# Zero products ahead of the first load, markers on the loads of x and table d, and two engines for the first-stage copies

## The chip, the core and the metric

The program runs on one core of a Trainium2 chip. A core has a matrix engine (TensorE, PE in the profile, with its weight loads as PEld), VectorE (DVE), ScalarE (ACT), GpSimd (POOL) and SyncE (SP), each with a queue of its own that it works through in order. They meet through semaphores. SP, ACT and POOL can also issue DMAs; the transfers of all three run on the core's 16 DMA engines. The metric is the device time of one execution in microseconds. The kernel before took 459.18 us, the median of 3 runs (457.12 to 460.07).

## What is computed

Two blocks follow each other. The first filters a sequence in the frequency domain, for 8 batches of 2496 rows and 256 columns:

```python
X = np.fft.rfft(x, axis=1)
F = (filt_r + 1j * filt_i)[None, :, :]
Y = X * F
y = np.fft.irfft(Y, n=x.shape[1], axis=1)
```

The second takes the 19968 rows of y as tokens for 8 experts. Each token goes to the expert with the largest logit; an expert keeps the 80 of its tokens with the largest gate, and the rows of all others stay zero:

```python
logits = x @ w_gate
expert_idx = np.argmax(logits, axis=1)
gate_w = probs[np.arange(N), expert_idx]          # softmax of the logits
h = np.maximum(x[tok_idx] @ w1[e], 0.0)           # tok_idx: the kept tokens of expert e
out[tok_idx] = gate_w[tok_idx, None] * (h @ w2[e])
```

All data is fp32.

## The kernel before, in words

A transform of length 2496 = 39 x 64 is done in two stages of matrix products. For each batch b:

- `load_x` (line 295) brings one **chunk** of x, 4 column groups of 117 rows and 256 columns (468 KB, the last of a batch 234 KB), on SP's queue. A batch has NCH = 6 chunks; the pool has NX0 = 7 slots. `put_x` loads the next chunk in the list of all 48; before the loop it is called seven times, with the first part of table d between the sixth and the seventh.
- `stage1(b, k)` (line 304) multiplies two groups of a chunk by the table `wf_t` in four calls, tile `pa` (line 311), and ACT copies the result into `t1` (line 317). A batch has NB = 11 blocks k; a chunk feeds two. `put_s1` issues the next block in the list and, when a chunk has been read to its end, calls `put_x`, so that a new chunk is loaded as soon as TensorE is through with an old one.
- `transpose1(b, u)` (line 319) turns part of `t1` through tile `pt`, and ACT copies it to `t2` (line 327). u runs over NU = 10.
- `stage2(b, u)` (line 331) multiplies `t2` by table `d_t` (tile `pb`, line 336). Two multiplications on DVE (line 344) take the filter `ft`, and two additions on POOL (line 351) combine them.
- `turn(b, u)` (line 355) turns the result back and adds the gate columns through `gi` (tile `py`, line 360). ACT copies the spectrum to SBUF (line 376), and after every second u it stores 512 KB of it to `yf` in DRAM (line 379). For the first two batches the spectrum also stays in SBUF, and only a fallback for unusual inputs reads their `yf`. DVE moves the gate columns (lines 382, 383).

The filter comes in five parts v. `load_filter(v, half)` (line 270) fetches 2 x 128 rows with indirect DMAs that POOL issues (line 273), `sign_filter(v)` (line 281) flips signs on ACT, and `turn_filter(v, k)` (line 284) turns a half through tile `pf` (line 289), which DVE copies to `ft` (line 291).

The order on each engine is written out by hand under `tc.manual_schedule()` (line 797); instructions stand on each queue in the order of the calls. First come the loads and all eleven blocks of batch 0, with parts 1 to 3 of table d loaded after blocks 2, 5 and 8. Then the first filter part is turned, two transposes and two blocks of batch 1 follow, and part 4 of d. The main loop (line 869) runs over v = 10 b + u in steps: `stage2` of step v, a filter part if it is due, `transpose1` of step v + 2, one block of the first stage (a second one when u = 3), zero rows of the output from batch 1 on, and `turn` of step v - 2. On POOL, a copy to `mark` (line 831) holds back the gathers of filter parts 1 and 2 until the last chunk of batch 0 is there.

Three PSUM slots (pool `fps`, tag f) serve `pa`, `pt` and `pb`, one (`pkps`) serves `pf`, two serve `py`. After the loop come the picking of tokens, the second transform of the picked rows and the experts; the change does not touch them.

## Time and profile before

| | before |
|---|---|
| median of 3 runs | 459.18 us (457.12 to 460.07) |
| the profiled execution | 462.53 us, span 460.7 us |
| mean granted TensorE clock | 0.983 |
| PE busy | 433.7 us (94%) |
| PEld busy | 410.1 us (89%) |
| ACT busy | 222.4 us (48%) |
| DVE busy | 188.4 us (41%) |
| POOL busy | 180.1 us (39%) |
| DMA | 109.96 MB, mean 239 GB/s |

The profile is one execution, recorded by the hardware. A busy line in slices cuts the span into 40 equal parts and gives the busy share of each in tenths. A row of the stretches gives the same in microseconds for a chosen time. A row of the waits reads: engine, tile and line that waited, what ended the wait, microseconds in total, times, the longest. A row of the timeline gives the start, the length, the engine, the line, the operation, the tiles written and read, and how many of them are merged. "remote" stands for a wait whose end the profile cannot give to an instruction. The ends of products are modelled, and some records can be missing. An fp32 product of one tile leaves two records, so a block of the first stage has eight.

### The profile page before, as it was taken

To read this page: it belongs to the slowest core of one execution; us is meant where nothing else is said; L and a number is where in the kernel's file an instruction comes from. 1 tells how busy PE (TensorE), PEld (TensorE's weight loads), DVE (VectorE), ACT (ScalarE), POOL (GpSimd) and SP (SyncE) were. 2 spreads that over 40 slices of the span, in tenths; PEclk is the share of its full clock that TensorE was granted. 3 is DMA by queue.
4 is the path that set the end of the run, shared out by engine and by line. 5 is a ranking of instruction groups with operands and counts; after the bars stand their busy time and mean duration, and the time that the engine had idled before them with its cause. 6 is when DMAs were issued, how large, how long until landed. Compare 5 with 4: busy or idle time off the path is not lost. (4 is left out here: it accounts for less than half of the span.)

```text
span 460.7 us, 8667 instructions
## 1 busy us (share of the span) xinstructions
PE 433.7 (94%) x3380; PEld 410.1 (89%) x3380; DVE 188.4 (41%) x550; ACT 222.4 (48%) x363; POOL 180.1 (39%) x246
## 2 busy tenths in 40 slices
PE   4969999999999999999999999999999999999990
PEld 4869899999999999999999998888888888888870
DVE  2134554544664454674545789568220000101100
ACT  2836667666676766667666754442123321111110
POOL 8468434343344433444443465420654002211210
PEclk9979999999999999999999999999999999999996
DMA  7996647877877887787894222797988991999200
GB/s 217 275 269 178 202 122 239 278 245 237 272 220 248 281 267 241 234 270 235 305 400 184 82 105 92 273 364 275 349 333 317 373 333 38 362 372 371 59 19 11
DMA packets 39477, 109.96 MB, mean 239 GB/s; under 512 B 5073, under 2 KB 14608, under 8 KB 38658
## 3 DMA queue, kind: packets, MB, share of 16 engines
q1 hardware_dynamic: 28688, 76.41, 50.7%
q10 hardware_dynamic: 6178, 21.04, 11.5%
q0 software_dynamic: 4560, 11.86, 7.9%
q8 instruction: 29, 0.48, 0.4%
q14 instruction: 22, 0.18, 0.1%
HBM read 68.97 MB, written 43.20 MB: 243 GB/s over the span
## 5 line engine op out<-in xcount | busy, mean ns | idle before, releaser
L351 POOL TENSOR_TENSOR p<-p,p 128x256 f32<-128x256 f32 x154 | 110.1, 736 | 138.6 <-DVE p L344 120.7
L344 DVE TENSOR_TENSOR p<-pb,ft 128x512 f32<-128x512 f32 x160 | 102.2, 681 | 19.5 <-PE pb L336 9.7
L317 ACT COPY t<-pa 128x480 f32<-128x480 f32 x88 | 87.0, 1001 | 27.8 <-PE pa L311 21.6
L311 PE MATMUL pa<-wf_t,x 117*128 117x120 f32 x704 | 93.6, 282 | 6.2 <-DMA x<-in_x_dram 6.0
L311 PEld LDWEIGHTS pa<-wf_t,x 117*128 117x128 f32 x704 | 87.9, 198 | 6.4 <-DMA x<-in_x_dram 6.0
L336 PE MATMUL pb<-d_t,t 128*128 128x128 f32 x640 | 86.2, 278 | 3.7 <-DVE p L344 3.5
L360 PE MATMUL py<-gi,p 128*128 128x136 f32 x640 | 87.8, 280 | 1.3 <-POOL p L351 0.7
L336 PEld LDWEIGHTS pb<-d_t,t 128*128 128x128 f32 x640 | 78.8, 193 | 4.7 <-issue 3.7
L360 PEld LDWEIGHTS py<-gi,p 128*128 128x128 f32 x640 | 79.8, 190 | 1.7 <-POOL p L351 1.0
L327 ACT COPY t<-pt 128x512 f32<-128x512 f32 x80 | 46.9, 587 | 67.1 <-PE pt L325 62.9
L508 PE MATMUL po<-yb,wt 128*128 128x256 f32 x240 | 56.6, 380 | 1.5 <-ACT wt L501 1.5
L508 PEld LDWEIGHTS po<-yb,wt 128*128 128x128 f32 x240 | 43.4, 190 | 6.5 <-ACT wt L501 1.7
L382 DVE COPY z<-py 128x16 f32<-128x16 f32 x60 | 11.2, 187 | 91.7 <-ACT ysp L376 57.9
L325 PE MATMUL pt<-ident,t 128*128 128x128 f32 x320 | 48.5, 274 | 0.0
L501 ACT COPY wt<-pw 128x512 f32<-128x512 f32 x39 | 22.8, 587 | 48.9 <-PE pw L496 42.5
L325 PEld LDWEIGHTS pt<-ident,t 128*128 128x128 f32 x320 | 38.0, 142 | 0.0
L376 ACT COPY ysp<-py 128x512 f32<-128x512 f32 x60 | 35.4, 590 | 0.0
L1153 PEld LDWEIGHTS ph<-xs,w 128*128 128x128 f32 x256 | 29.7, 192 | 1.7 <-DVE xs L1144 1.1
L1153 PE MATMUL ph<-xs,w 128*128 128x80 f32 x256 | 29.8, 274 | 0.8 <-DVE xs L1144 0.8
L1168 PE MATMUL po<-w,hT 128*80 128x256 f32 x128 | 28.8, 379 | 0.0
L1168 PEld LDWEIGHTS po<-w,hT 128*80 128x80 f32 x128 | 18.6, 150 | 7.5
L479 POOL DMA_INDIRECT gts<-rows_tbl,idxb x16 | 16.2, 1010 | 21.0 <-DVE idxb L695 16.7
(200 smaller groups left out, 315.6 us busy)
## 6 DMA issues: line engine op xcount, KB each, us to landing
out_dram<-zero_t SPq DMA_DIRECT2D x64, 312.0 KB
x<-in_x_dram SPq DMA_DIRECT2D x40, 468.0 KB
w<-in_moe_w_dram SPq DMA_DIRECT2D x16, 1024.0 KB
yf<-ysp ACTq DMA_DIRECT2D x30, 512.0 KB
yb<-yf SPq DMA_DIRECT2D x6, 2560.0 KB
yf<-ys ACTq DMA_DIRECT2D x10, 512.0 KB
x<-in_x_dram SPq DMA_DIRECT2D x8, 234.0 KB
d_t<-d_tbl SPq DMA_DIRECT2D x5, 256.0 KB
```

The costliest lines, as they stand in the source:

```text
L311: nc.tensor.matmul(out=ps[:, i, :, 2 * NS * cb:2 * NS * cb + 2 * NS], lhsT=xt[0:NJ * N1, (2 * k + i) % JC, 128 * cb:128 * cb + 128], rhs=w ...
L317: nc.scalar.copy(out=t1[:, 2 * k - h:2 * k - h + 2], in_=ps[:])
L325: nc.tensor.transpose(ps[:, i, cb, :], t1[:, a:a + 2, :].rearrange("p r n -> p (r n)"), ident[:])
L327: nc.scalar.copy(out=t2[:].rearrange("p i c -> p (i c)"), in_=ps[:].rearrange("p i c q -> p (i c q)"))
L336: nc.tensor.matmul(out=ps[:, cb, i], rhs=d_t[:, 2 * u + i, :], start=True, stop=True, lhsT=t2[:, i, 128 * cb:128 * cb + 128])
L344: nc.vector.tensor_tensor(out=pt, in0=ps[:].rearrange("p c s r q -> p (c s) r q"), in1=f.unsqueeze(2).to_broadcast([128, 2 * NDB, 2, NQ]), ...
L351: adder.tensor_tensor(out=yt[:, :, r, :], in0=yt[:, :, r, :], in1=pr[1][:, :, 1 - r, :], op=op)
L360: nc.tensor.matmul(out=ps[:, i, ZW * cb:ZW * cb + ZW], rhs=gi[:, cb, :], lhsT=yt[:, 2 * cb + i].rearrange("p r q -> p (r q)"), start=True, ...
L376: nc.scalar.copy(out=dst.rearrange("p s (h w) -> p s h w", h=2), in_=pv[:, :, :, 0:128])
L508: nc.tensor.matmul(pos[t][:, 0, 0:C], lhsT=wts[t, g // 2][:, g % 2, i, :], rhs=ybs[t][:, s, :], start=(s == 0), stop=(s == NS - 1))
L1153: nc.tensor.matmul(ph[:, fc // 4, fc % 4, 0:cap], lhsT=self.w1s[e][:, k, 128 * fc:128 * fc + 128], rhs=xs[:, k, :], start=(k == 0), stop=( ...
L1168: nc.tensor.matmul(po[0:cap, :], lhsT=hT[:, fc, :], rhs=self.w2s[e][:, fc, :], start=(fc == 0), stop=(fc == NFC - 1))
```

## The change

1. Line 113: a bf16 tile `warm` is set to zero by DVE as its first work, and TensorE multiplies it by itself nine times (128 x 512 results into one slot of `fps`) ahead of its first product of x.
2. In the first stage of batch 0, blocks 1, 4, 7 and 10 are copied by DVE instead of ACT.
3. The two small loads of the gate columns move from POOL's queue to ACT's, ahead of the loop; the mark on POOL waits for chunk 3 of batch 0 instead of the last.
4. A chunk of x is no longer loaded when a slot comes free. `put_x(v)` is called once in a step; it loads as many chunks as are free and due. Chunks 7 to 20 in the list have a step each before which they are not due. Up to step 19, DVE writes one element of the slot first (a marker), so that the DMA on SP's queue waits until DVE has come to that place in its order. Part 1 of d is loaded after block 7, parts 2 to 4 in steps 0, 2 and 4, each behind such a marker.
5. The first filter part gets its sign after block 6. Before the loop there is one block of batch 1 instead of two; step 7 does one more. `turn_filter` comes after the step's first-stage block instead of before the transpose, and its second half uses `fps`.
6. The five stores of batch 0's spectrum are issued in step u = 4 of batches 1 to 5 instead of during batch 0.

```diff
@@ -110,6 +110,8 @@
     consts = ctx.enter_context(tc.tile_pool(name="consts", bufs=1))
     dpool = ctx.enter_context(tc.tile_pool(name="dram", bufs=1, space=DRAM))
 
+    warm = consts.tile([128, 128], BF16, name="warm")
+    nc.vector.memset(warm[:], 0.0)
     ident = consts.tile([128, 128], F32, name="ident")
     make_identity(nc, ident)
     ident_bf = consts.tile([128, 128], BF16, name="ident_bf")
@@ -179,6 +181,7 @@
 
 
     NE, NY, NO = 3, 2, 3
+    NWARM = 9
     yf = {b: dpool.tile([128, NS, C], F32, name=f"yf_{b}") for b in range(B)}
     ypool = ctx.enter_context(tc.tile_pool(name="spec", bufs=NY))
     ysb = {}
@@ -283,7 +286,8 @@
 
         def turn_filter(v, k):
             f = fst[:, v]
-            ps = pkps.tile([128, 2, NDB, 128], F32, name=f"pf_{k}_{v}", tag="k")
+            ps = (fps if k else pkps).tile([128, 2, NDB, 128], F32, name=f"pf_{k}_{v}",
+                                           tag="f" if k else "k")
             for i in range(2):
                 for cb in range(NDB):
                     nc.tensor.transpose(ps[:, i, cb, :],
@@ -292,8 +296,10 @@
                 out=ft[k][:, 2 * v:2 * v + 2].rearrange("p u c s q -> p u c (s q)"),
                 in_=ps[:])
 
-        def load_x(b, ch):
+        def load_x(b, ch, hold=False):
             xt = xpool.tile([128, JC, C], F32, name=f"x_{b}_{ch}", tag="x")
+            if hold:
+                nc.vector.memset(xt[0:1, 0, 0:1], 0.0)
             ng = min(JC, NG - JC * ch)
             nc.sync.dma_start(
                 out=xt[0:NJ * N1, 0:ng, :],
@@ -314,7 +320,8 @@
                         rhs=wf_t[:], start=True, stop=True)
             h = k // (NB - 1)
             t1 = st["t1", b][:, :, h:h + N2 - 1].rearrange("p a (j g) -> p g j a", j=NJ)
-            nc.scalar.copy(out=t1[:, 2 * k - h:2 * k - h + 2], in_=ps[:])
+            copy = nc.vector.tensor_copy if b == 0 and k % 3 == 1 else nc.scalar.copy
+            copy(out=t1[:, 2 * k - h:2 * k - h + 2], in_=ps[:])
 
         def transpose1(b, u):
             t1 = st["t1", b]
@@ -352,6 +359,10 @@
                                     in1=pr[1][:, :, 1 - r, :], op=op)
             st["yt", b, u] = yt
 
+        def keep_spectrum(b, u):
+            src = st["ys"] if b >= NY else ysb[b][:, 2 * u - 2:2 * u + 2, :]
+            nc.scalar.dma_start(out=yf[b][:, 2 * u - 2:2 * u + 2, :], in_=src)
+
         def turn(b, u):
             yt = st.pop(("yt", b, u))
             ps = yps.tile([128, 2, 512], F32, name=f"py_{b}_{u}", tag="y")
@@ -374,9 +385,10 @@
             if b >= B - 2:
                 nc.scalar.copy(out=zz, in_=pv[:, :, :, 128:ZW])
             nc.scalar.copy(out=dst.rearrange("p s (h w) -> p s h w", h=2), in_=pv[:, :, :, 0:128])
-            if u % 2 == 1:
-                src = st["ys"] if b >= NY else ysb[b][:, 2 * u - 2:2 * u + 2, :]
-                nc.scalar.dma_start(out=yf[b][:, 2 * u - 2:2 * u + 2, :], in_=src)
+            if u % 2 == 1 and b > 0:
+                keep_spectrum(b, u)
+            if u == 4 and 0 < b < 6:
+                keep_spectrum(0, 2 * b - 1)
             if b < B - 2:
                 zz = zz[:, :, 0, :]
                 nc.vector.tensor_copy(out=zz, in_=pv[:, :, 0, 128:ZW])
@@ -798,29 +810,44 @@
             nc.scalar.dma_start(out=frow, in_=frow_dram.ap())
             nc.scalar.dma_start(out=wf_t, in_=wf_dram.ap())
             nc.scalar.dma_start(out=fsig, in_=fsig_dram.ap())
+            for cb in range(NDB):
+                nc.scalar.dma_start(out=gi[:, cb, 128:128 + E],
+                                    in_=moe_w_gate[128 * cb:128 * cb + 128, :])
+            pre = fps.tile([128, 4, 128], F32, name="warm_ps", tag="f")
+            for _ in range(NWARM):
+                nc.tensor.matmul(out=pre[:], lhsT=warm[:], start=True, stop=True,
+                                 rhs=warm[:].unsqueeze(1).to_broadcast([128, 4, 128]))
             xs = [(b, ch) for b in range(B) for ch in range(NCH)]
             s1 = [(b, k) for b in range(B) for k in range(NB)]
 
-            def put_x():
-                if xs:
-                    load_x(*xs.pop(0))
+            held = dict(zip(range(NX0, NX0 + 14),
+                            (-1, 0, 2, 3, 4, 5, 7, 8, 11, 13, 15, 16, 17, 18)))
+            free = [NX0]
+
+            def put_x(v):
+                while xs and free[0] and held.get(B * NCH - len(xs), -1) <= v:
+                    load_x(*xs.pop(0), hold=v < 20)
+                    free[0] -= 1
 
             def put_s1():
                 if s1:
                     b, k = s1.pop(0)
                     stage1(b, k)
                     if (2 * k + 2) % JC == 0 or k == NB - 1:
-                        put_x()
+                        free[0] += 1
 
             def load_d(g):
+                if g:
+                    nc.vector.memset(d_t[0:1, SG * g, 0:1], 0.0)
                 nc.sync.dma_start(out=d_t[:, SG * g:SG * g + SG, :],
                                   in_=d_dram.ap()[:, SG * g:SG * g + SG, :])
 
             for _ in range(NCH):
-                put_x()
+                load_x(*xs.pop(0))
             load_d(0)
             for _ in range(NX0 - NCH):
-                put_x()
+                load_x(*xs.pop(0))
+            free[0] = 0
             load_filter(0, 0)
             load_filter(0, 1)
             for t in (lg, zero_t, *zs, key, kt):
@@ -828,24 +855,23 @@
             nc.gpsimd.tensor_copy(out=gi[:, 0, 0:128], in_=ident[:])
             nc.gpsimd.tensor_copy(out=gi[:, 1, 0:128], in_=ident[:])
             mark = tpool.tile([1, 1], F32, name="mark")
-            nc.gpsimd.tensor_copy(out=mark[:], in_=st["x", 0, NCH - 1][0:1, 0, 0:1])
+            nc.gpsimd.tensor_copy(out=mark[:], in_=st["x", 0, NCH - 3][0:1, 0, 0:1])
             load_filter(1, 0)
-            nc.gpsimd.dma_start(out=gi[:, 0, 128:128 + E], in_=moe_w_gate[0:128, :])
-            nc.gpsimd.dma_start(out=gi[:, 1, 128:128 + E], in_=moe_w_gate[128:256, :])
             load_filter(1, 1)
             load_filter(2, 0)
             load_filter(2, 1)
             for k in range(NB):
                 put_s1()
-                if k in (2, 5, 8):
-                    load_d(k // 3 + 1)
-            sign_filter(0)
-            turn_filter(0, 0)
-            turn_filter(0, 1)
+                if k == 6:
+                    sign_filter(0)
+                if k == 7:
+                    load_d(1)
+                    put_x(-1)
+            for k in range(2):
+                turn_filter(0, k)
             for v in range(LEAD):
                 transpose1(0, v)
-                put_s1()
-            load_d(4)
+            put_s1()
             nlow = max(128 - cap, 8) // 8
             n0 = max(128 - cap, 8) // 8
             early = {67: [lambda: pick_edge(0, 6, 8, -1.0)],
@@ -870,10 +896,11 @@
                 b, u = divmod(v, NU)
                 if b < B:
                     stage2(b, u)
-                    if v + 2 < NU:
-                        if v % 2 == 1:
-                            sign_filter(v // 2 + 1)
-                        turn_filter(v // 2 + 1, v % 2)
+                    if v + 2 < NU and v % 2 == 1:
+                        sign_filter(v // 2 + 1)
+                    put_x(v)
+                    if v in (0, 2, 4):
+                        load_d(2 + v // 2)
                     if v < 4:
                         load_filter(3 + v // 2, v % 2)
                     elif v == 4:
@@ -883,8 +910,10 @@
                     if w < B * NU:
                         transpose1(*divmod(w, NU))
                     put_s1()
-                    if u == 3:
+                    if u == 3 or v == 7:
                         put_s1()
+                    if v + 2 < NU:
+                        turn_filter(v // 2 + 1, v % 2)
                     if b > 0:
                         put_zeros(1)
                 if v >= LATE:
```

## The prediction

> **What bounds the kernel now.** I read, in order, the page's slices, busy time by stretch, the waits of the first 110 us, the first-stage products in two stretches, and the timeline. In the slices each digit is tenths of 11.5 us.
>
> ```profile
> PE   4969999999999999999999999999999999999990
> PEclk9979999999999999999999999999999999999996
> ```
>
> TensorE (PE) is full from the fourth slice to the end, except the third and at the start; only the third shows a lower granted clock. The stretches say how much work each holds (length, then busy us and records of PE, weight load, DVE, ACT, POOL, then clock, DMA share, GB/s):
>
> ```profile
> 5.97:18.77 12.80, 12.80 (x90) 12.80 (x91) 0.00 (x0) 9.19 (x10) 7.42 (x14) 1.00 0.92 283
> 18.77:23.50 4.73, 3.75 (x32) 3.32 (x31) 1.38 (x2) 3.46 (x7) 3.82 (x5) 1.00 0.94 272
> 23.50:35.67 12.17, 8.31 (x50) 7.68 (x48) 3.77 (x6) 4.03 (x7) 7.71 (x10) 0.72 0.91 268
> 35.67:60.00 24.33, 23.66 (x203) 22.50 (x202) 12.69 (x28) 16.00 (x25) 15.30 (x21) 1.00 0.56 172
> 60.00:120.00 60.00, 60.00 (x533) 60.00 (x533) 28.99 (x74) 39.54 (x59) 24.35 (x35) 1.00 0.76 234
> ```
>
> The undisturbed rate is the last row's: 533 products in 60 us, 8.9 per us. Between 23.50 and 35.67 there are 50, 4.1 per us. So the kernel is bound by TensorE from about 60 us on, and what a change of the opening can win is what the opening loses against 8.9 per us. DMA is at 0.91 to 0.94 of its time from 6 to 36 us: the opening is crowded with loads. The waits (us in total, times, longest):
>
> ```profile
> PE pa L311 <- DMA x<-in_x_dram: 6.0, 1, 6.0
> PE pb L336 <- DVE p L344: 3.5, 1, 3.5
> DVE p L344 <- remote: 7.5, 1, 7.5
> POOL mark L831 <- DMA x<-in_x_dram: 4.6, 1, 4.6
> PE pf L289 <- ACT fst L281: 1.4, 3, 1.0
> ```
>
> PE waits 6.0 us for the first chunk of x, and 3.5 us (27.2 to 30.7) for VectorE (DVE), which itself stood 7.5 us for something the profile cannot name. ACT's next copy also restarted only then (29.38 against DVE's 29.26), though PE's records have the products done by 25.8. The mark, which waits for the last chunk of batch 0, shows when that landed: it ran at 16.18. The first-stage rows in two stretches, 6 to 11.5 and 12.5 to 18.6 (count, shortest/median/longest ns, first and last start):
>
> ```profile
> L311 PEld LDWEIGHTS pa<-wf_t,x x27: 288/333/338, 6.0 to 11.5; 117*128 117x128 f32 x27
> L311 PE MATMUL pa<-wf_t,x x26: 397/421/569, 6.0 to 11.5; 117*128 117x120 f32 x26
> L311 PE MATMUL pa<-wf_t,x x57: 275/275/275, 12.2 to 18.5; 117*128 117x120 f32 x57
> ```
>
> 26 starts in 5.5 us is 0.212 us each; 57 in 6.3 us is 0.1125. A block k has eight: 1.70 us early, 0.90 later. The page's clock says 1.0 in both, so it does not record the state before its first event.
>
> [...] 421 ns becomes 275 at about 11.7 us, and the 1-us stretches put the second half-clock spell at 28.8 to 35.6, 6.8 us[...]. [...] from 12 to 20 us, with almost no gather, SP's queue has 87.9% of DMA time; from 24 to 30, beside gathers, 59.5% against their 33.2%. [...]
>
> **The change, part by part,** against the profiled execution: 462.53 us, span 460.70.
>
> *Warm-up.* [...] They need only DVE's memset, so they run[...], in PE's 6.0 us of waiting: cost 0 while the cover stands. [...] Gain at most 26 x (0.212 - 0.1125) = 2.6 us, and 0 if zeros or the 1 us gap leave the clock cold.
>
> *x sets the pace.* With a warm clock eleven blocks need 9.9 us and would end at 15.9, but the last chunk lands at 16.2. The trace's semaphore records, which no view prints, put the chunks at 5.9, 7.3, 10.6, 13.1, 15.2 and 16.1. Two blocks per chunk: 10.7 to 12.5, 13.1 to 14.9, 15.2 to 17.0, the last to 17.9. Before, it ended at 18.77. So 0.9 of the 2.6 is left.
>
> *Copies by two engines.* ACT's copy takes 0.99 and ACT finished at 19.84; then came the sign (0.89), for which PE waited 1.0. Now block 10 is DVE's: the 128x512 copy of the same kind is 0.69, so 18.7, and the sign is done at block 6. Turns of the filter, 2 x 0.44, run to 18.8: transposes start at 18.8 instead of 20.86, 2.0 earlier. DVE was idle from 4.4 to 19.25, so four copies cost nothing.
>
> *Filters earlier.* The mark now waits for chunk 3 (13.1, not 16.18), and gathers start 3.2 us sooner. A gather is 131 KB per 1.27 us of POOL, 0.10 MB/us; 3.2 us of that is 0.33 MB, or 1.2 us at 0.28 MB/us, which x(1,0) lands later: 20.4 becomes 21.6. Transposes end at 19.7, so PE waits 1.9 and block (1,0) ends at 22.5. Second-stage product (0,0) starts at 22.5; before, 23.51, less the 0.89 of one first-stage block that now runs at step 7: 22.6. **Up to here 0.1 is won;** the start's gain turns into a wait for x.
>
> *The stall.* From product (0,0) to (0,2) before took 23.51 to 35.77, 12.3 us, for two steps of 0.89 + 0.44 + 0.44 + 0.89 = 2.66. Lost: 6.9, of which 3.5 idle, about 2.5 at half clock (30.7 to 35.6 at half), the rest waiting for sign and filter rows. After: filter rows are 3 us ahead and the turns follow the first-stage block, x(1,1) and its table part are 0.73 MB at the 0.18 left beside the gathers, 4 us, so about 25.6 against a need at 26.5. Product (0,2) at 27.8, like for like 34.9 before: **7.0 won.**
>
> *Steps 2 to 9.* 203 products at 8.9 per us are 22.8 us; the stretch took 24.33, 1.5 lost, mostly to turns behind the sign. I take half, 0.7 (0 to 1.5).
>
> *Held x.* A marker is a one-element memset (DVE's shortest rows, 0.14) behind that step's two multiplications. It waits for a slot already read, so nothing queues behind it on DVE but filter copies and z; on SP the next d load and zero store wait with it. Steps are 3.15 us:
>
> ```profile
> 60.07 1.05 PE L336 MATMUL pb<-d_t,t 128*128 128x128 f32 x8
> 61.39 1.05 PE L311 MATMUL pa<-wf_t,x 117*128 117x120 f32 x8
> 63.22 1.05 PE L336 MATMUL pb<-d_t,t 128*128 128x128 f32 x8
> ...
> 61.21 1.28 DVE L344 TENSOR_TENSOR p<-pb,ft 128x512 f32<-128x512 f32 x2
> ```
>
> Marker at about 62.6, need two steps on at 61.39 + 6.30 = 67.7: 5.1 us for the chunks issued at steps 15 and 16; for those of 11 and 13 an extra block makes it 6.1; others have three steps. The semaphore records have x landing 4.5 to 6.9 us after issue between 60 and 140 us, mostly 5.0 to 5.5. Cost 0 to 2 x 1.8 = 3.6; I take 0.4.
>
> *First spectrum later.* Five 512 KB stores (0.33 of ACT each) leave 45 to 75 us and come at u = 4 of batches 1 to 5: 0.52 MB per 32 us or 16 GB/s more on 234. Only the fallback reads them. Nothing, in the gaps of ACT (39.54 of 60 us busy); uncovered 5 x 0.33 = 1.6. Four table markers: nothing, their parts are needed two to four steps later.
>
> Sum: -7.0 - 0.7 + 0.4 = -7.3: 455.2 for the profiled execution. It stands 3.35 above the median, and the three runs lie 3 us apart, wider than the rest of the kernel can explain, so I take the stall and half clock (6.0) as varying, absent in the fastest run (457.12) and worth 459.18 - 457.12 = 2.1 in the median. Without it about 1.0 of the stall would remain as a wait for the sign. So 7.3 - 6.0 + 1.0 = 2.3 in any run, plus 2.1: **4.4, or 454.8.** The fastest run less 2.3 gives the same.
>
> **Rivals.** (1) *The stall is in every run* and the 3.35 is the recording's: 459.18 - 7.3 = 451.9. For it: all of it happens under a DMA at 0.98 to 1.00. Against it: the spread of the runs. Chance 0.22. (2) *The clock does not hold.* Waiting for x leaves PE some 50 to 80% busy from 9 to 16, with 1.9 us idle before block (1,0)[...]. For it: the spell at 28.8 followed a window only half busy. Against it: the 1.0 us gap at 19.2 did not lower it. It includes that zeros do not warm at all. Chance 0.20. (3) *Slower: held chunks come late.* Place: the four chunks with two steps. If all land L after issue, PE waits 2(L - 5.1) + 2(L - 6.1); 4.4 is eaten at L = 6.7, and L = 8 gives 9.6, 464.4. For it: 6.9 occurs, and these loads meet zero and spectrum stores. Against it: mostly 5.0 to 5.5. Chance 0.13. The likeliest has 0.45, its own range 453.2 to 456.6.
>
> **Numbers.** A measurement of this kernel tells about 1%, 4.6 us. Under 454.6 lie rival 1 and half of the likeliest, a little less: 0.45; over 463.8 most of rival 3: 0.12; within: 0.43. The range 451.3 to 460.3 leaves out rival 3's bulk and the edges.
>
> **What would show it.** First-stage products at 275 ns from the start (else the warm-up fails); pb's first record near 22.5 and pb of step 2 near 28; no 3.5 us wait of pb for p; the granted clock 1.0 throughout 20 to 40; PE waits for x at block (1,0) of about 1.9, and at steps 13 to 18 under 1. Wrong if x waits at those steps add to over 4, or if the stall stands elsewhere.

## The result, and the profile after

Ten executions of the changed kernel took 453.86 us in the median (452.77 to 455.07). Ten of the kernel before, among them the three that the prediction knew, took 457.39 (456.02 to 460.84). The ratio is 0.9907, 95% interval 0.988 to 0.9934, so 3 to 5.5 us or about 1% faster. Medians here and below are of all executions, while a ratio leaves out those more than 1.5% above the fastest of their kernel. The forecast of 454.8 is 0.9 above what came; as a gain it was 4.4 on a median of 459.18, and 3.5 came on one of 457.39. A second set, on the chip called 3 below, gave 452.87 against 458.72, 0.9876 (0.9833 to 0.9918).

The profiled execution of the changed kernel took 453.17 us, span 451.4, mean granted clock 0.993. The slices of its page:

```profile
PE   7899999999999999999999999999999999999990
PEclk9999999999999999999999999999999999999997
```

The dip of TensorE in the third slice is gone, and so is the lower clock there. By stretch of time, cut as before (columns: length, then busy us and records of PE, weight load, DVE, ACT, POOL, then clock, DMA share, GB/s):

```profile
5.97:18.77 12.80, 11.40 (x96) 10.90 (x96) 7.67 (x29) 7.58 (x9) 9.24 (x16) 1.00 0.92 275
18.77:23.50 4.73, 4.13 (x36) 3.68 (x35) 2.30 (x5) 2.34 (x4) 3.76 (x4) 1.00 0.87 262
23.50:35.67 12.17, 12.17 (x111) 12.14 (x110) 7.49 (x18) 9.41 (x15) 10.08 (x13) 1.00 0.64 186
35.67:60.00 24.33, 24.33 (x218) 24.27 (x217) 13.70 (x37) 17.10 (x26) 13.45 (x19) 1.00 0.48 141
60.00:120.00 60.00, 59.33 (x522) 58.88 (x521) 30.02 (x89) 39.23 (x58) 24.66 (x36) 1.00 0.81 275
```

From 23.50 to 35.67 there are 111 products, 9.1 per us, where there were 50. The next stretch holds 218 instead of 203, and only the last holds fewer, 522 instead of 533: the held loads take something back there. The DMA share falls from 0.91 to 0.64 in the third stretch and rises to 0.81 in the last. Of the waits of TensorE before 110 us, these are the larger ones (us in total, times, longest):

```profile
PE pa L317 <- DMA x<-in_x_dram: 3.0, 4, 1.1
PE warm_ps L818 <- DVE warm L114: 1.0, 1, 1.0
PE pt L332 <- DVE t L324: 0.4, 1, 0.4
```

The waits for `p` and for the sign are not among them. The timeline of TensorE shows where the rest lies (start, length, what runs, and in brackets the idle time before and what ended it):

```profile
1.00 3.81 PE L818 MATMUL warm_ps<-warm 128*128 128x512 bf16 x9 [1.00 <-DVE warm L114]
5.90 4.29 PE L317 MATMUL pa<-wf_t,x 117*128 117x120 f32 x32 [1.09 <-DMA x<-in_x_dram]
10.52 2.02 PE L317 MATMUL pa<-wf_t,x 117*128 117x120 f32 x16 [0.33 <-DMA x<-in_x_dram]
13.47 4.70 PE L317 MATMUL pa<-wf_t,x 117*128 117x120 f32 x40 [0.93 <-DMA x<-in_x_dram]
...
19.40 1.06 PE L332 MATMUL pt<-ident,t 128*128 128x128 f32 x8 [0.36 <-DVE t L324]
20.70 1.15 PE L317 MATMUL pa<-wf_t,x 117*128 117x120 f32 x8 [0.24 <-ACT t L334]
21.69 1.06 PE L343 MATMUL pb<-d_t,t 128*128 128x128 f32 x8
...
27.03 1.06 PE L343 MATMUL pb<-d_t,t 128*128 128x128 f32 x8
```

The zero products fill 1.0 to 4.8. Then x sets the pace with three waits of 0.3 to 1.1. From the second-stage product (0,0) at 21.69 on, TensorE runs without a gap; product (0,2) stands at 27.03.

In the profile of before, the products of steps 0, 1 and 2 stand at these places:

```profile
23.51 1.08 PE L336 MATMUL pb<-d_t,t 128*128 128x128 f32 x8
...
30.69 2.05 PE L336 MATMUL pb<-d_t,t 128*128 128x128 f32 x8 [3.50 <-DVE p L344]
...
35.77 1.06 PE L336 MATMUL pb<-d_t,t 128*128 128x128 f32 x8
```

Between fixed products the two profiles differ as follows. "pb n" is the start of the second-stage product of step n in the timeline of TensorE. Before, two blocks of batch 1 stand ahead of pb 0; after, one, and the other (0.89) lies between pb 2 and pb 10.

| us | before | after | gain |
|---|---|---|---|
| start to pb 0 | 23.51 | 21.69 | 1.8 |
| pb 0 to pb 2 | 12.26 | 5.34 | 6.9 |
| pb 2 to pb 10 | 30.60 | 29.84 | 0.8 |
| pb 10 to pb 20 | 32.88 | 33.83 | -0.95 |
| pb 20 to the end | 361.5 | 360.7 | 0.8 |

The sum is 9.3, the difference of the spans, and more than the 3.5 of the medians. What of it is the change and what is that one profile had to be found out.

### The profile page after: what moved, and what is told of

It is laid out like the page before. It is cut to its first block, busy times and chain, and to the rows that moved or that the text cites. A ratio compares the mean times of both kernels' runs of the same rounds, so it can differ in the third digit from the quotient of the medians.

```text
span 451.4 us, 8713 instructions
## 1 busy us (share of the span) xinstructions
PE 431.9 (96%) x3389; PEld 406.6 (90%) x3389; DVE 194.2 (43%) x577; ACT 219.5 (49%) x359; POOL 178.5 (40%) x244
## 5 line engine op out<-in xcount | busy, mean ns | idle before, releaser
L324 ACT COPY t<-pa 128x480 f32<-128x480 f32 x84 | 83.8, 1002 | 26.1 <-PE pa L317 25.7
L317 PE MATMUL pa<-wf_t,x 117*128 117x120 f32 x704 | 91.2, 276 | 3.4 <-DMA x<-in_x_dram 3.0
L317 PEld LDWEIGHTS pa<-wf_t,x 117*128 117x128 f32 x704 | 84.9, 192 | 5.1 <-DMA x<-in_x_dram 1.8
L343 PE MATMUL pb<-d_t,t 128*128 128x128 f32 x640 | 85.2, 276 | 0.2
L394 DVE COPY z<-py 128x16 f32<-128x16 f32 x60 | 11.2, 187 | 86.6 <-ACT ysp L387 57.9
L1197 PE MATMUL po<-w,hT 128*80 128x256 f32 x128 | 28.8, 379 | 0.0
L1197 PEld LDWEIGHTS po<-w,hT 128*80 128x80 f32 x128 | 18.6, 150 | 7.5
L1188 DVE TENSOR_SCALAR hT<-ph 128x320 f32<-128x320 f32 x8 | 3.9, 491 | 47.9 <-ACT hT L1187 47.9
```

Source lines behind the costliest of these rows:

```text
L317: nc.tensor.matmul(out=ps[:, i, :, 2 * NS * cb:2 * NS * cb + 2 * NS], lhsT=xt[0:NJ * N1, (2 * k + i) % JC, 128 * cb:128 * cb + 128], rhs=w ...
L324: copy(out=t1[:, 2 * k - h:2 * k - h + 2], in_=ps[:])
L343: nc.tensor.matmul(out=ps[:, cb, i], rhs=d_t[:, 2 * u + i, :], start=True, stop=True, lhsT=t2[:, i, 128 * cb:128 * cb + 128])
L1197: nc.tensor.matmul(po[0:cap, :], lhsT=hT[:, fc, :], rhs=self.w2s[e][:, fc, :], start=(fc == 0), stop=(fc == NFC - 1))
```

## The experiments

The theory: the opening of the old kernel loses its time between pb 0 and pb 2 and in the steps up to 9, because filter rows, signs and turns come too late in a crowded queue of loads; the order of the loads and the place of the turns win it back. Rivals: the warm-up wins it; the copies on VectorE win it; the 6.9 us are an accident of one profile. The runs stand on three chips, so segments between products are compared as well as times. Chips 2, 3 and 10 are the names used here; the kernel before took 458.55, 458.72 and 462.7 us on them. Which chip the first profiles of before and after come from is not on record.

**The kernel before once more.** No edit.

> The kernel before, once more, for a second profile of it. Theory (the long stall at 27.2 to 30.7 us and the half clock after it belong to some executions only): ratio 1.00; in this profile product (0,0) to (0,2) of the second stage takes 7 to 9 us instead of 12.3, TensorE waits 1 to 2 us for sign and filter rows there, the granted clock stays 1.0, and the span is 455 to 457. Rival (the stall is part of the kernel): it stands again with 3 us or more and a half-clock spell, span 459 to 461.

458.37 us on chip 2, 0.9998 (0.9972 to 1.0024). The profiled execution, 458.31, lies near the median, and its profile is another than the first one: pb 0 to pb 2 takes 9.43 instead of 12.26, and VectorE's 7.5 us of "remote" are not there. The timeline of TensorE:

```profile
23.44 1.08 PE L336 MATMUL pb<-d_t,t 128*128 128x128 f32 x8
...
26.98 0.44 PE L289 MATMUL pf<-ident,fst 128*128 128x128 f32 x2 [2.10 <-DMA fst<-in_filt_r_dram,frow]
...
29.10 1.93 PE L336 MATMUL pb<-d_t,t 128*128 128x128 f32 x8
...
32.87 1.06 PE L336 MATMUL pb<-d_t,t 128*128 128x128 f32 x8
...
37.71 0.44 PE L289 MATMUL pf<-ident,fst 128*128 128x128 f32 x2 [0.19 <-ACT fst L281]
```

Here the turn of the filter waits 2.1 us for its rows, in front of products that could run. The product at 29.10 is slow (1.93 for eight records instead of 1.06), and the granted clock is 0.50 there. The stretches of this profile show that:

```profile
24.60:28.00 3.40, 1.30 (x11) 1.06 (x11) 1.79 (x3) 0.14 (x2) 2.66 (x3) 1.00 0.95 274
28.00:31.40 3.40, 3.40 (x18) 3.38 (x17) 0.48 (x2) 2.15 (x4) 2.91 (x5) 0.50 0.89 260
31.40:35.00 3.60, 3.60 (x35) 3.60 (x34) 2.58 (x5) 1.69 (x3) 2.92 (x4) 1.00 0.93 263
```

So an execution near the median loses 4.1 us between pb 0 and pb 2 (9.43 less the 5.34 of the changed kernel): the wait of 2.1, some 1.5 at half clock (18 records in 3.4 us where the next 3.6 hold 35), and a rest of 0.5, put down to the sign. The other 2.8 of the first profile are not in this one. The half clock is not in every execution either: this one has a mean granted clock of 0.987, and nine of the fourteen have 0.990 or more.

**No warm-up.** Without the zero products.

```diff
-            pre = fps.tile([128, 4, 128], F32, name="warm_ps", tag="f")
-            for _ in range(NWARM):
-                nc.tensor.matmul(out=pre[:], lhsT=warm[:], start=True, stop=True,
-                                 rhs=warm[:].unsqueeze(1).to_broadcast([128, 4, 128]))
```

> The changed kernel without the nine products of the zeroed tile. Theory (arrival of x paces the first stage): early products at 421 ns[...], but the first stage ends 0.2 to 1.0 us later than with them; 454.4, between 454.0 and 455.2. Rival (the clock at the start is the gain): the whole 2.6 us come back, 456.5 or more.

453.97 us on chip 2, 0.990 (0.9864 to 0.9935); the changed kernel had 0.9907 and 0.9876. In the profile the clock is full at 9.1 us instead of 4.5 by the clock records (the products from 5.5 to 11.2 take 382 ns in the median, where 275 stood), and pb 0 starts at 24.20; from there on the segments are those of the changed kernel (5.35 and 29.84). In these two profiles the warm-up does what it says (it does not in all: see the run with loads free), but whether it shortens an execution these times can't tell: the kernel with late filters, below, has the warm-up and took 452.91 on the same chip, and the two intervals overlap. The bulk of the gain is not from here.

**x free.** A chunk of x is loaded as soon as a slot is free, as before the change; the parts of d keep their new places and markers.

```diff
-                while xs and free[0] and held.get(B * NCH - len(xs), -1) <= v:
-                    load_x(*xs.pop(0), hold=v < 20)
+                while xs and free[0]:
+                    load_x(*xs.pop(0))
...
                         free[0] += 1
+                        put_x(0)
...
-                    put_x(-1)
...
-                    put_x(v)
```

> The changed kernel with x loaded as soon as a slot is free, without markers, as in the kernel before; the parts of table d keep their markers. Theory (the order of the loads is the gain): the DMA engines stay over 0.9 busy until 35 us, filter rows and x(1,0) land 1 to 3 us later, TensorE waits again in the first steps; 455.9, between 455 and 457.5. Rival (the holding does nothing, filters earlier and later turns suffice): 453.9, and the one wait of 0.65 at 85 us goes.

460.03 us on chip 2 (454.25 to 463.98), 1.0004 (0.9977 to 1.0031). All of the gain is gone in the median; two of the 22 executions, at 454.3 and 454.4, still have it. But the timeline of TensorE, from an execution of 461.16, shows a reason of this kernel's own:

```profile
33.46 2.04 PE L343 MATMUL pb<-d_t,t 128*128 128x128 f32 x8 [5.65 <-DMA d_t<-d_tbl]
```

Part 1 of d is issued after block 7 and now stands on SP's queue behind five chunks of x; TensorE waits 5.7 for it and then runs at half clock for 6.8 us by the trace's clock records, which no view prints (granted 0.86 from 23.5 to 35.67 and 0.93 from there to 60); that is why pb 2 to pb 10 is long here too (32.67) although the turns are late. Neither kernel has this order of the loads, so the run does not say that holding x is what wins.

**Late filters.** The mark on POOL waits for the last chunk of batch 0 again.

```diff
-            nc.gpsimd.tensor_copy(out=mark[:], in_=st["x", 0, NCH - 3][0:1, 0, 0:1])
+            nc.gpsimd.tensor_copy(out=mark[:], in_=st["x", 0, NCH - 1][0:1, 0, 0:1])
```

> The changed kernel with the mark of the kernel before: the gathers of filter parts 1 and 2 wait for the last chunk of batch 0 (16.1 us) instead of chunk 3 (13.3 us). Theory: rows of parts 1 and 2 come 2.7 us later; with turns behind the first-stage block half of that is covered; 454.6, between 453.9 and 456. Rival (the gathers beside x cost what they win, x of batch 0 lands earlier without them): 453.4.

452.91 us on chip 2, 0.9884 (0.9844 to 0.9925): no loss. pb 0 to pb 2 is 5.34. With the gathers as late as before, no product waits for filter rows.

**The changed kernel once more, on chip 3.** No edit.

> The changed kernel once more, as the reference of this group on one chip. All theories: ratio 0.988 to 0.993 to the kernel before, no wait of TensorE over 1.2 us after 6 us.

452.87 us, 0.9876 (0.9833 to 0.9918). The profiled execution is the slowest of its six, 455.5. The stretches of its trace tell why:

```profile
4.20:7.60 3.40, 2.39 (x18) 1.86 (x16) 0.00 (x0) 1.20 (x2) 2.79 (x4) 1.00 0.95 253
7.60:11.10 3.50, 1.54 (x14) 1.42 (x13) 3.31 (x7) 0.52 (x2) 3.50 (x7) 1.00 0.98 244
11.10:17.90 6.80, 6.56 (x31) 6.30 (x30) 3.16 (x21) 2.71 (x3) 2.52 (x5) 0.50 0.86 252
17.90:25.00 7.10, 6.50 (x57) 6.05 (x56) 3.09 (x6) 4.64 (x7) 5.27 (x7) 1.00 0.73 216
```

A wait of 1.96 us for x leaves TensorE busy for 1.54 of 3.5 us, and then the clock is half for 6.8 us; pb 0 comes at 25.07. After that the segments are the usual ones (5.33, 29.84, 33.12).

**Loads free.** x is loaded as in the run with x free, and d at its old places (after blocks 2, 5, 8 and ahead of the loop); no markers at all. The turns stay late.

```diff
-                if k == 7:
-                    load_d(1)
-                    put_x(-1)
+                if k in (2, 5, 8):
+                    load_d(k // 3 + 1)
...
             put_s1()
+            load_d(4)
...
-                    put_x(v)
-                    if v in (0, 2, 4):
-                        load_d(2 + v // 2)
```

> The changed kernel with x loaded when a slot is free and the parts of table d at the places of the kernel before (after blocks 2, 5 and 8, part 4 ahead of the loop), no markers; all else as changed. In the run with only x free, part 1 of d stood behind five chunks of x and TensorE waited 5.7 us for it, so that run joined two things; this one parts them. Theory (order of the loads is the gain): DMA over 0.9 busy until 35 us, waits of 2 to 4 us in total for filter rows, x or d in the first four steps, ratio 0.995 to 1.00. Rival (the loss there was part 1 of d alone; clock, copies and turns carry the gain): no such waits, ratio 0.990.

453.22 us on chip 3, 0.9881 (0.9837 to 0.9926): no loss. Its stretch from 23.5 to 35.67:

```profile
23.50:35.67 12.17, 12.17 (x111) 12.14 (x110) 7.50 (x13) 9.44 (x15) 9.98 (x12) 1.00 0.90 264
```

TensorE has no gap while the DMA is as full as before the change, 0.90. So holding the loads is not needed for the gain, and the theory that their order wins it falls in this form.

This profile shows something of the warm-up too. The nine zero products are there, from 0.99 to 5.0, but the first-stage products after them are slow. First those of the changed kernel, then those of this run, in the stretch from 5.4 to 9.2 (count, shortest/median/longest ns, first and last start):

```profile
L317 PE MATMUL pa<-wf_t,x x25: 274/275/371, 5.9 to 9.0; 117*128 117x120 f32 x25
```

```profile
L317 PE MATMUL pa<-wf_t,x x15: 421/421/569, 6.0 to 9.1; 117*128 117x120 f32 x15
```

By the trace's clock records the clock is full only at 10.43 us here, and at 10.29 in the run with all copies on ACT; in the other seven profiles with the zero products it is full at 3.9 to 5.6.

**Loads only.** The opposite: x and d held, copies by two engines and spectrum later; but no warm-up, the mark late, and `turn_filter` ahead of the transpose as before.

```diff
-                    if v + 2 < NU and v % 2 == 1:
-                        sign_filter(v // 2 + 1)
+                    if v + 2 < NU:
+                        if v % 2 == 1:
+                            sign_filter(v // 2 + 1)
+                        turn_filter(v // 2 + 1, v % 2)
...
-                    if v + 2 < NU:
-                        turn_filter(v // 2 + 1, v % 2)
```

> The changed kernel without the warm-up, with the mark of the kernel before and with the filter turned ahead of the transposes as before: left are the held loads of x and d, the copies by two engines and the late stores of the first spectrum. Theory: most of the gain, ratio 0.990 to 0.993; turns wait for the sign some 1 to 2 us in total. Rival (parts work together, earlier filter rows and later turns are needed to remove the waits): ratio over 0.995.

457.02 us on chip 3, 0.9966 (0.9949 to 0.9983): a quarter of the gain. pb 0 to pb 2 takes 6.20, and pb 2 to pb 10 32.22, which is 2.4 more than with late turns. The timeline of TensorE shows the step (the first line is in step 1, the second in step 3; steps 5 and 7 have the same 0.19):

```profile
27.80 0.83 PE L293 MATMUL pf<-ident,fst 128*128 128x128 f32 x4 [0.47 <-ACT fst L284]
...
34.68 0.84 PE L293 MATMUL pf<-ident,fst 128*128 128x128 f32 x4 [0.19 <-ACT fst L284]
```

A turn ahead of the transpose stands at the head of TensorE's queue until ACT has signed the second row block; behind the first-stage block it finds it done. In step 1 the turn starts 1.54 after `pb` (26.26) instead of 0.89, and the transpose 0.66 after the turn instead of 0.44: 0.87, which is 6.20 less 5.33. In steps 3, 5 and 7 these two and the next gap lose some 0.75 each, 2.3 of the 2.4.

**Chunks one step earlier.** The mark late, and two held chunks due at steps 14 and 15 instead of 15 and 16.

```diff
-                            (-1, 0, 2, 3, 4, 5, 7, 8, 11, 13, 15, 16, 17, 18)))
+                            (-1, 0, 2, 3, 4, 5, 7, 8, 11, 13, 14, 15, 17, 18)))
```

> The changed kernel with the gathers of filter parts 1 and 2 behind the last chunk of batch 0 and two chunks of x due one step earlier, where one wait of 0.65 us stood at 85.7 us. Theory: x of batch 0 lands sooner and nothing later is late, 1.0 to 1.6 us under the changed kernel run beside it. Rival (the gain of late gathers was the spread of runs and chips): within 0.5 us of it.

452.88 us on chip 3, against 452.87 of the changed kernel there. pb 10 to pb 20 is 32.94, and no product waits for x in it. That segment is 33.12 in the run of the changed kernel on this chip, so there was 0.2 to win, too little to be seen. No kernel here is measurably faster than the changed one.

**Turns early, alone.** The diff of the turns from above on the changed kernel, nothing else.

> The changed kernel with the filter turned ahead of the transposes, as in the kernel before; all else as changed. New theory (the gain is the place of the turns): in each of the four odd steps TensorE stands 0.35 to 0.65 us for the sign and loses 0.2 more while the two halves of the turn drip in, 2.6 us in all; ratio 0.993 to 0.997. First theory (order of the loads) and the clock: 0.988 to 0.990, since both are left in.

465.84 us on chip 10, 1.0057 (1.0037 to 1.0077). pb 2 to pb 10 is 32.29, 2.45 longer than in the changed kernel, as in the other run with early turns. pb 0 comes only at 29.80, which is not from the turns, since the diff touches nothing ahead of it: see what follows the last run.

**Late turns without the rest.** Loads free, no warm-up, the mark late, and all first-stage copies on ACT; left of the change are the late turns with the moved block, the early sign, the gate loads on ACT and the spectrum.

```diff
-            copy = nc.vector.tensor_copy if b == 0 and k % 3 == 1 else nc.scalar.copy
-            copy(out=t1[:, 2 * k - h:2 * k - h + 2], in_=ps[:])
+            nc.scalar.copy(out=t1[:, 2 * k - h:2 * k - h + 2], in_=ps[:])
```

> The changed kernel without the warm-up, without held loads, with the mark of the kernel before and all first-stage copies on ACT: left are the later turns, the sign after block 6, one block of batch 1 moved to step 7, the gate loads on ACT and the late stores. New theory: 2.6 us for the turns and up to 1 for the early sign, ratio 0.991 to 0.994; the rest of the change's gain is the start (clock, copies, earlier filter rows). Rival (the start gives nothing, x paces it): 0.988 to 0.990, as the whole change.

461.64 us on chip 10, 0.9976 (0.9959 to 0.9993). pb 2 to pb 10 is 29.88, the full gain of the late turns. But pb 0 to pb 2 is 11.53. In the timelines of VectorE and ACT the stall of the first profile is back, at the same place:

```profile
29.26 1.29 DVE L350 TENSOR_TENSOR p<-pb,ft 128x512 f32<-128x512 f32 x2 [8.13 <-remote]
```

```profile
29.32 0.58 ACT L333 COPY t<-pt 128x512 f32<-128x512 f32 x1 [3.35 <-remote]
```

TensorE's timeline has the products that they wait for done at 23.6 and 24.0, 5.3 us and more before, and the two engines take up work 0.06 us apart.

**All copies on ACT, alone.** The same diff on the changed kernel.

> The changed kernel with all first-stage copies on ACT. In the profile of the changed kernel a copy takes 0.98 to 1.00 us on either engine and DVE's last one starts at 18.27, when ACT's is done at 18.30. So both theories: 0 to 0.5 us more, ratio 0.988 to 0.992. If two engines matter, the transposes start over 1 us later and the ratio is over 0.992.

461.56 us on chip 10, 0.9974 (0.9955 to 0.9992). pb 0 comes at 27.71 after transposes that start at 22.57, with 4.0 of "remote" on ACT in between; pb 2 to pb 10 is 30.40. So this run does not settle what the copies are worth. Its timeline of VectorE shows something else that they do:

```profile
0.88 0.06 DVE L840 MEMSET d_t<- 1x1 f32 x1
...
10.24 0.06 DVE L302 MEMSET x<- 1x1 f32 x1
```

In the changed kernel both markers run at 16.46, behind the third copy of VectorE. Without the copies nothing holds VectorE, so part 1 of d is released at 0.9 us and the chunk at 10.2. These markers are only as late as the work ahead of them on VectorE.

**Held longer.** Five of the held chunks due one step later.

```diff
-                            (-1, 0, 2, 3, 4, 5, 7, 8, 11, 13, 15, 16, 17, 18)))
+                            (-1, 0, 2, 3, 4, 5, 7, 8, 12, 14, 16, 17, 18, 18)))
```

> The changed kernel with chunks 15 to 19 of x due one step (3.15 us) later. It prices the hold: the window from marker to need falls from 5.3 to 2.15 us for three of them and from 6.2 to 3.05 for one, and x lands about 5 us after issue. If the window is read rightly: waits of 2 and 3 x 2.9 us at steps 13 to 18, 10.7 in all, ratio 1.008 to 1.013. If the DMAs had slack (landings under 3 us when needed): under 3 us in all, ratio below 0.996.

474.11 us on chip 10, 1.023 (1.0196 to 1.0264). pb 10 to pb 20 is 43.55, 9.7 more than in the changed kernel, and the timeline of TensorE shows why:

```profile
89.12 1.91 PE L317 MATMUL pa<-wf_t,x 117*128 117x120 f32 x8 [3.03 <-DMA x<-in_x_dram]
90.82 2.01 PE L371 MATMUL py<-gi,p 128*128 128x136 f32 x8
...
99.24 1.16 PE L317 MATMUL pa<-wf_t,x 117*128 117x120 f32 x5 [1.94 <-DMA x<-in_x_dram]
```

Three waits of 1.74, 3.03 and 1.94 are 6.7; the other 3.0 I put down to half clock behind the 3.0 us wait and the next (eight records in 2.01 us, a granted clock of 0.94 from 60 to 120 us). Due one step sooner, the same chunks cost the changed kernel 0.95 us in one profile and 0.2 in the other. The edge lies within one step.

**What the runs on chip 10 have besides their edits.** All four profiles from there show waits of 3.2 to 8.1 us on ACT or VectorE with the name "remote", between 17 and 30 us; none of the eight from chips 2 and 3 has one before 60 us. In the run just told, which is the changed kernel itself up to about step 11, VectorE stands 4.69 us with "remote" until 22.46, and pb 0 comes at 29.22 instead of 21.69 to 25.07 in the other profiles of the changed kernel:

```profile
22.46 0.96 DVE L324 COPY t<-pa 128x480 f32<-128x480 f32 x1 [4.69 <-remote]
```

So the changed kernel is not free of this stall, and the ratios of the other three runs on chip 10 mix it with their edits; only their segment pb 2 to pb 10 is used here. The changed kernel itself was not timed on that chip. I estimate that it would gain nothing there: the median of the held run, 474.11, less the 9.7 that the holding costs is 464.4, where the kernel before took 462.7. The cause stays open: DMA was at 0.85 to 0.97 of its time in the stretch from 18.8 to 23.5 in which they begin or stand, but so it was in the run with loads free (0.95), which has none.

The profiles in one table, in us (pb 2 to pb 10 holds one block more, 0.89, in all rows but the first two):

| run, chip | pb 0 | pb 0 to 2 | pb 2 to 10 | pb 10 to 20 | median, ratio |
|---|---|---|---|---|---|
| before, first profile | 23.51 | 12.26 | 30.60 | 32.88 | 457.39 |
| before, 2 | 23.44 | 9.43 | 30.49 | 32.89 | 0.9998 |
| after, first profile | 21.69 | 5.34 | 29.84 | 33.83 | 0.9907 |
| after, 3 | 25.07 | 5.33 | 29.84 | 33.12 | 0.9876 |
| no warm-up, 2 | 24.20 | 5.35 | 29.84 | 33.13 | 0.990 |
| late filters, 2 | 21.55 | 5.34 | 29.84 | 33.17 | 0.9884 |
| loads free, 3 | 22.95 | 5.33 | 29.85 | 32.94 | 0.9881 |
| chunks earlier, 3 | 22.71 | 5.34 | 29.85 | 32.94 | 0.9882 |
| x free, 2 | 22.31 | 11.15 | 32.67 | 32.94 | 1.0004 |
| loads only, 3 | 23.59 | 6.20 | 32.22 | 33.49 | 0.9966 |
| turns early, 10 | 29.80 | 7.70 | 32.29 | 33.11 | 1.0057 |
| late turns, 10 | 22.53 | 11.53 | 29.88 | 32.95 | 0.9976 |
| copies on ACT, 10 | 27.71 | 6.80 | 30.40 | 33.21 | 0.9974 |
| held longer, 10 | 29.22 | 6.29 | 30.03 | 43.55 | 1.023 |

## Why the prediction was right, and where its steps were not

**Where the gain is.** Between the second profile of before (chip 2) and the run with loads free (chip 3), neither with a remote stall, the spans differ by 5.15: 0.5 up to pb 0, 4.1 from pb 0 to pb 2, 0.6 from pb 2 to pb 10 (1.5 with the block that moved there, which takes as much from the start: 0.5 less 0.9 is -0.4), and 0 after. On chips 2 and 3 the timed gain was 4.6 to 5.9 us in the five kernels that keep late turns and part 1 of d ahead of x; in the first set it was 3.5. The forecast's 4.4 lies among these, and its place, from pb 0 to pb 9, was the right one. That it lies there is in part luck: the start was taken as 0.1 won where this pair has 0.4 lost, and steps 2 to 9 as 0.7 won where it has 1.5. On chip 10 the whole change has no measured gain at all.

**It is won more than once.** The prediction put the gain of pb 0 to pb 2 down to earlier filter rows and later turns together. With late turns, undoing the earlier filters (5.34) or the held loads (5.33) cost nothing there, and with early turns and late filters the held loads still saved most of that segment (6.20 against 9.43). So the held loads cure most of the wait alone, and late turns with earlier filters cure all of it. Whether late turns need the earlier filters for that is not shown: the one run with late turns and neither of the others (late turns without the rest, on chip 10) has the remote stall in that very segment. In steps 2 to 9 it is plainer. With the turns early, 2.4 is lost there both without the warm-up and the earlier filters (32.22) and with all the rest of the change in place (32.29); nothing else replaced the place of the turns.

**Warm-up and pace of x.** Right: products at 275 ns in the median from 5.9 on, and the turn of the filter follows the last block at 18.00, where 17.9 was worked out as its end. The cover that was named holds: the zero products take 3.81, from 1.00 to 4.81, and end 1.1 before x is there. That they would fit had been the author's estimate; nothing in the profile of before shows such a product. That a warm clock would shorten the start by more than x allows was rightly cut to 0.9; in the timed runs even that can't be told from nothing. The prediction allowed that zeros might not warm the clock; in two of nine profiles it was full only at 10.29 and 10.43 us, as told above.

**Copies by two engines.** Mis-sized. The copy was taken from another row at 0.69 and measures 0.96 to 1.00; the transposes start at 19.40 instead of 18.8 and wait 0.36 for it. "DVE was idle from 4.4 to 19.25, so four copies cost nothing" also missed that VectorE's constants now queue behind the first copy:

```profile
8.99 2.09 DVE L124 CAST iota<-iota_i 128x128 f32<-128x128 int32 x1
9.13 1.96 DVE L130 CAST lane<-lane_i 128x1 f32<-128x1 int32 x1
9.19 1.90 DVE L149 CAST trow<-trow_i 128x1 f32<-128x1 int32 x1
...
12.71 0.96 DVE L324 COPY t<-pa 128x480 f32<-128x480 f32 x1
```

These three took 0.44, 0.23 and 0.17 in the profile of before, at 1.6 to 1.9, beside POOL's operations of 0.1 to 0.3. Now they end together at 11.1, just as POOL's run of memsets (7.5 to 11.0, of 0.4 to 1.2 each) ends. Each cast outlasts several of the memsets; what makes the casts long was not shown, and no run here separates it. No product waited for it, since x was late anyway.

**"Up to here 0.1 is won".** This step failed. The delay of x(1,0) from earlier gathers was estimated at 1.2 us (to 21.6), with a wait of 1.9 in TensorE. The trace's semaphore records have the chunk at 18.6, and block (1,0) starts at 20.70 with no wait for x. pb 0 came at 21.69, not 22.5. The estimate let the gathers take their full rate from x, and the sum left out that part 1 of d and the chunk after it were now held behind block 7, which freed SP's queue at just that time. With the loads not held, the same chunk lands at 19.6 (x free) and 20.4 (loads free); with late filters, at 17.9. So the gathers cost 0.7 instead of 1.2, and holding wins 1.0 to 1.8. But no product waited for the chunk even at 20.4, since the transposes before it came later than the sum had them.

**The stall.** Product (0,2) was put at 27.8 and came at 27.03, 0.8 sooner, which is all from pb 0; pb 0 to pb 2 was 5.3 as worked out. Splitting the 6.9 lost into a varying and a standing part was what made the median come out right. Its size came out as well: 2.0 in any run (1.0 of the rest, 1.0 for the sign) and 2.1 for the median's share of the varying part make 4.1, and the second profile of before has 4.1. What that 4.1 is was not right. In that profile all of it is a wait for filter rows, the half clock after it and the sign; there is no remote stall in it, to which, with the half clock after it, the prediction gave 2.1. So the agreement in size is in part luck. The 2.1 rested on three executions; by the same rule the ten give 457.39 less 456.02, or 1.4. Not right either was where the stall varies: the prediction thought from run to run, and the runs show it above all from chip to chip (all four profiles of chip 10, none of chips 2 and 3, and the first one of before).

**Steps 2 to 9.** Half of the lost 1.5 was taken; all of it was won, 1.65 in the first pair (0.76 + 0.89).

**Held x.** Taken as 0.4; the segment lost 0.95 in the first profile and 0.2 to 0.6 in the others with the same places (33.11 to 33.49 against 32.88). The lines show the step as it was worked out: the marker of step 16 at 79.57 on VectorE, and block 85.66 behind it on TensorE.

```profile
79.57 0.06 DVE L302 MEMSET x<- 1x1 f32 x1
```

```profile
85.66 1.12 PE L317 MATMUL pa<-wf_t,x 117*128 117x120 f32 x8 [0.65 <-DMA x<-in_x_dram]
```

The chunk landed 5.8 us after its issue at 79.72 by the semaphore records, in a window of 5.3: a little over the middle of the range that was read from before. It was one of the two chunks named as the tightest; the other one was in time. Rival 3 (464) was therefore near: held one step longer, it came true with 9.7 us. That 10.7 was expected is near by luck: 10.7 was for waits alone, of which 6.7 came, and the half clock that adds 3.0 was not in that sum.

**The other rivals.** Rival 1, 451.9, falls with the second profile of before, which has no remote stall. Rival 2, the clock that does not hold, did happen in the second profile of the changed kernel, which has 2.3 us more of span than the first profile. There TensorE had worked 1.54 of 3.5 us before the clock fell; in the second profile of before it was 1.30 of 3.4, and in the spell that the prediction names, at 28.8 in the first profile of before, 1.57 of 3.4 (25.4 to 28.8).

**Spectrum and markers of d.** Nothing was expected, and no wait for either shows. No run took them away by themselves, nor the early sign or the new place of the gate loads.

## What to carry to other kernels

Put an operation that waits for another engine behind independent work of the same step on its own engine's queue; here, on chip 3, having the turn of the filter ahead of that work cost 0.9 and 2.4 us of a gain of 5.9. When several parts of a change may cure the same wait, undoing each of them alone can show nothing: take them away together, and compare segments between fixed instructions rather than times. Before a stall in one profile goes into a sum at its full size, look for it in a second execution, best on another chip, above all if its end has no name in the trace.

## What the runs showed that was not expected

- In two profiles the clock fell to half behind a stretch of 3.4 or 3.5 us with 1.30 or 1.54 us of work in it; the longest wait was 2.10 and 1.96 us. It stayed half for 3.4 us once and 6.8 us once, and a wait of 2 us so cost some 1.5 more in the one profile and up to 3.3 in the other (31 records in 6.8 us, which take 3.5 at 0.1125 each). The share of work alone does not decide it: in the run with late turns without the rest, a stretch with 1.49 us of TensorE's work held the clock (22.5 to 26.0; the eight records at 26.02 took 1.15). By the clock records of the first profiles, the changes of the clock lie 17.07, 6.83 and 416.43 us apart before and 440.32 after: 5, 2, 122 and 129 times 3.4133.
- Behind the products of a zeroed tile the clock was full at 3.9 to 5.6 us in seven of the nine profiles that have them; in the first run without them it was full at 9.1. In the other two it was full only at 10.29 and 10.43. In the seven, the 3.4 us just before the step held 2.8 us or more of TensorE's work; in the two, the two stretches of 3.4 us that end 3.4 us before the step held 2.0 to 2.6 each. What decides between them was not shown.
- A VectorE copy of 128x480 fp32 from PSUM into the strided places of `t1` takes 0.96 to 1.00 us where 128x512 into a plain row takes 0.69.
- Three casts of VectorE took 1.9 to 2.1 us beside memsets of POOL, 0.17 to 0.44 at their earlier place, in the kernel before and in the run with all copies on ACT.
- On one of the three named chips, ACT and VectorE start up to 5.7 us after the work they wait for is recorded as done, in every profile taken there, and the kernel before is 4 us slower on it. Open.
